# Attention scores with positive sign, high parts as plain copies, eight heads' query copies on GpSimd, loads of values and weights spaced

## The chip, the cores and the metric

The kernel runs on one core of a Trainium2 chip. The metric is device time in microseconds (us) of one execution, as the median of several runs. The core has TensorE (PE in the profile, with its weight loads as PEld), VectorE (DVE), ScalarE (ACT), GpSimd (POOL) and SyncE (SP, which here issues nearly all DMAs).

## The reference

Attention with a cumulative gate, then a dense mixture of eight experts whose gate is balanced by eight Sinkhorn steps:

```python
scores = scale * np.matmul(q, k.transpose(0, 1, 3, 2))        # 4 batches, 8 heads, 576 rows, 64 wide
cum = np.cumsum(np.maximum(s, 0.0), axis=-1)
bias = -(cum[:, :, :, None] - cum[:, :, None, :])
scores = np.where(causal, -1000000000.0, scores + np.minimum(bias, 0.0))
attn = np.exp(scores - np.max(scores, axis=-1, keepdims=True))
attn = attn / (np.sum(attn, axis=-1, keepdims=True) + 1e-09)
x = attn @ v                                                  # to 2304 rows of 512
P = np.exp(x @ w_gate - max)                                  # 8 rounds: rows, then columns to sum 1
for e in range(8):
    out += P[:, e:e + 1] * (np.maximum(x @ w1[e], 0.0) @ w2[e])   # 512 -> 1024 -> 512
```

## The kernel before

All products run in a rounded fp32 form (fp32r); a number is kept as a high part and a low part (its rest), and a product is built from high times high, high times low and low times high.

**Attention** takes the first 350 us. There are 32 heads in 16 groups of two (group g holds heads 2g and 2g+1), and a group has five slots of 128 query rows (the last has 64 of both heads). The loop over `ti` starts slot `ti` (`st0`: scores on TensorE, row minimum on VectorE in `row_min`, exponential on ScalarE), and in the same pass does later steps of earlier slots: `st1` scales by the reciprocal row sum, `st2` transposes on TensorE and copies to SBUF on VectorE, `st3` multiplies with the values `vt` into `pv`. Scores are held with a minus sign, so that the maximum is a minimum; the mask adds 8e9.

**A head is prepared** in `prep_head(h)`, called in slots 1 and 3 of the group before its own. Its raw queries and keys (`rawq`, `rawk`, each 64 rows loaded twice, into partitions 0 to 63 and 64 to 127) become: `qa` (line 418, VectorE: minus the queries, rounded, on 128 partitions; for odd heads as two instructions of 512 and 64 columns), `ka` (line 423, VectorE: the keys times a column `sgn` of +1 and -1), then the low parts on GpSimd (line 428 into `kb`, line 432 into the upper half of `qa`), and a DMA `qb<-qa` (line 426) that copies the high part of the queries. Four rows of the gates reach `qb` and `kb` by small DMAs (lines 413, 416). The buffers `qa0` to `qa3` serve head h as number h mod 4. `load_head(h + 2)` (lines 334, 335) follows.

**Values** are loaded by `load_v(g + 1)` (lines 446, 449) into one of two buffers `vt`, in slot 3 of group g; the buffer must be free of the `pv` products of group g - 1.

**Weights of the early experts' pieces** are loaded as `wraw` (line 616, two loads of 512 KB for a piece u) and split into high parts on ScalarE (line 110) and low parts on GpSimd (line 111). For the first two pieces this is done in slots 4 to 17 of the loop: both loads in the first of seven slots, the four splits in the last four.

**The rest** (350 us to the end) is the experts' work in a scheme of products of sums of blocks (lines 962, 1083, 1138 for the matmuls).

A scheduler orders the instructions of each engine when the program is built, by its own estimate of durations, so an edit in one place can move instructions of all engines near it. Each engine and the SP queue then run their instructions strictly in that order; one that waits holds up all behind it.

Of the kernel before, what the change touches and what calls it, by code (L numbers as in the profile page):

```python
# [8 lines left out]
F32 = mybir.dt.float32  # L9
F32R = mybir.dt.float32r  # L10
AF = mybir.ActivationFunctionType
ALU = mybir.AluOpType
AX = mybir.AxisListType

P = 128
B, H, S, D = 4, 8, 576, 64
# [8 lines left out]
MASKED = 8e9  # L25
# [20 lines left out]
def fused_kernel(ctx: ExitStack, tc: tile.TileContext, qT, kT, v, s, w_gate, wu, out):  # L46
    nc = tc.nc

    const = ctx.enter_context(tc.tile_pool(name="const", bufs=1))
# [57 lines left out]

    def split(dst, lo, src, eng=None):

        nc.scalar.copy(dst, src)  # L110
        (eng or nc.gpsimd).tensor_tensor(
            out=lo, in0=src, in1=dst.bitcast(F32), op=ALU.subtract
        )

    def split_piece(u, pc, raw):
        if pc % 2 == 0:
            t = "w1" if pc < 2 else "w2"
            wts[u, t] = wpool.tile([P, 2, 1024], F32R, name=t, tag=t)
        w = wts[u, "w1" if pc < 2 else "w2"]
        sl = slice(pc % 2 * 512, (pc % 2 + 1) * 512)  # L120
        split(w[:, 0, sl], w[:, 1, sl], raw)

# [206 lines left out]
    def load_head(h):  # L329
# [12 lines left out]

    sgn = const.tile([P, 1], F32, name="sgn")
    nc.gpsimd.memset(sgn[:D], 1.0)
    nc.gpsimd.memset(sgn[D:], -1.0)

    crow_d = dram.tile([B * H, 6, S], F32, name="crow_d")
    cum = apool.tile([B * H, S], F32, name="cum", tag="T", bufs=7)
    cr = stage.tile([B * H, 6, S], F32R, name="cr", tag="w7")
    nc.gpsimd.memset(cr[:, 0:2, :].bitcast(F32), 1.0)  # L350
    nc.gpsimd.memset(cr[:, 4:6, :].bitcast(F32), -1.0)
    nc.vector.tensor_scalar(
# [13 lines left out]
        out=mask,  # L366
        in_=mask,
        compare_op=ALU.is_ge,
        fill=MASKED,
        base=384,  # L370
# [31 lines left out]
    def prep_head(h):  # L402
# [9 lines left out]
        for i, o, n in at:  # L412
            nc.sync.dma_start(
                out=qb[D : D + 4, o : o + n].bitcast(F32), in_=rows[:, 2:6, i : i + n]
            )
        nc.sync.dma_start(out=kb[D : D + 4, :].bitcast(F32), in_=rows[:, 0:4, :])
        for i, o, n in at:
            nc.vector.tensor_scalar(
                out=qa[:, o : o + n], in0=rq[:, i : i + n], scalar1=-1.0, scalar2=None,
                op0=ALU.mult,  # L420
            )
        with tc.issue_after(gates_done.ins) if h < 2 else ExitStack():
            nc.vector.tensor_scalar(
                out=ka, in0=rk, scalar1=sgn[:, 0:1], scalar2=None, op0=ALU.mult
            )
            nc.sync.dma_start(out=qb[:D].bitcast(F32), in_=qa[:D].bitcast(F32))
            lo = nc.vector if h < 2 else nc.gpsimd
            lo.tensor_tensor(
                out=kb[:D], in0=rk[:D], in1=ka[:D].bitcast(F32), op=ALU.subtract
            )  # L430
            for i, o, n in at:
                lo.tensor_tensor(
                    out=qa[D:, o : o + n], in0=rq[D:, i : i + n],
                    in1=qa[D:, o : o + n].bitcast(F32), op=ALU.add,
                )
# [28 lines left out]
    def row_min(T, sc, m, init, out):  # L464
        nc.vector.tensor_tensor_reduce(
            out=T, in0=sc, in1=m, scale=0.125, scalar=init,
            op0=ALU.add, op1=ALU.min, accum_out=out,
        )
# [148 lines left out]

    def w_split_early(u, pc):
        split_piece(u, pc, wraw[pc // 2][:, pc % 2 * 512 : (pc % 2 + 1) * 512])

# [45 lines left out]
    for ti in range(NS + 3):  # L666
        if ti < NS:
            g, i = slots[ti]
            if i == 3 and g + 1 < NG:
                load_v(g + 1)  # L670
            for j in heads(slots[ti]):
                st0(slots[ti], j)
# [21 lines left out]
        if 4 <= ti < 18:  # L694
            u, r = divmod(ti - 4, 7)
            if r == 0:
                w_load_early(u)
            elif r > 2:
                w_split_early(u, r - 3)
# [611 lines left out]
```

## Time and profile before

| | |
|---|---|
| median of 3 runs | 1742.1 us (1740.54 to 1746.08) |
| profiled execution, its own time | 1738.24 us |
| its span, first to last instruction | 1736.5 us |
| PE busy | 1682.0 us (97%) |
| DVE busy | 1238.2 us (71%) |
| ACT busy | 838.3 us (48%) |
| POOL busy | 855.8 us (49%) |
| mean granted TensorE clock | 0.994 of full speed |

The profiled execution's time is its span and 1.74 us around it. Busy shares are means over very different stages, so the table says which engine is the widest, not where time is lost.

### The profile page before, as it was taken

The numbers are of one execution on the slowest core, as the hardware profiler recorded it, in microseconds if no ns is written. First come the engines' busy times: TensorE is split into PE (matmuls) and PEld (weight loads), VectorE is DVE, ScalarE is ACT, GpSimd is POOL, SyncE is SP. The second block draws the span as 40 slices with busy tenths as digits, with TensorE's granted clock in tenths as the row PEclk, the third lists the DMA queues.
The fourth block names the chain that finished last, engine by engine and source line by source line (L and its number), as shares of the span: only waits on it lengthen the run. The fifth ranks groups of instructions, "written<-read, shape, count | busy, mean of one in ns | idle before, by whom it ended". The sixth has DMA issues, their size and how long they took to land.

```text
span 1736.5 us, 31221 instructions
## 1 busy us (share of the span) xinstructions
PE 1682.0 (97%) x11109; PEld 1574.6 (91%) x11109; DVE 1238.2 (71%) x2352; ACT 838.3 (48%) x1817; POOL 855.8 (49%) x761
## 2 busy tenths in 40 slices
PE   5889999999999999999999999999999999999998
PEld 4678888889889889998889999999999999999998
DVE  6867666565586766776548777877776787777775
ACT  5876666723554444444245444444445444444442
POOL 5559647612564543553314445544544454454454
PEclk9899999999999999999999999999999999999999
DMA  6667656364687767865956555565587555555552
GB/s 177 195 195 221 204 161 200 104 235 176 212 314 255 244 209 239 260 220 189 336 184 193 178 187 183 183 191 178 184 307 256 177 183 188 180 182 182 186 176 85
DMA packets 204986, 352.09 MB, mean 203 GB/s; under 512 B 21088, under 2 KB 103008, under 8 KB 204800
## 3 DMA queue, kind: packets, MB, share of 16 engines
q1 hardware_dynamic: 204512, 349.52, 62.6%
q8 instruction: 88, 1.44, 0.3%
q10 hardware_dynamic: 320, 0.59, 0.1%
q14 instruction: 66, 0.54, 0.1%
HBM read 249.94 MB, written 94.81 MB: 199 GB/s over the span
## 4 chain that ended last, share of the span: by engine, by line
PE 78%; DVE 11%; DMA 4%; issue 3%; POOL 2%; SPq 1%; ACT 1%; DVEq 0%; POOLq 0%; ACTq 0%
PE c L962 29%; PE zz L1083 13%; PE zz L1138 12%; PE y L1138 8%; PE g L148 3%; PE g L177 3%; DVE s L937 3%; PE sc L456 2%; PE pv L558 2%; DVE h L252 2%; PE tr L528 2%; PE c L148 2%; PE c L177 2%; DVE a L1066 1%; DVE z L255 1%
## 5 line engine op out<-in xcount | busy, mean ns | idle before, releaser
L252 POOL TENSOR_TENSOR w2o<-r,w2o 128x512 fp32r<-128x512 f32 x196 | 279.6, 1448 | 363.9 <-ACT w2o L1119 327.6
L962 PE MATMUL c<-xS,w1o 128*128 128x384 f32 x1344 | 278.0, 339 | 4.2 <-DVE z L255 1.7
L1138 PE MATMUL zz<-w2o,h 128*128 128x256 f32 x2016 | 280.2, 282 | 0.0
L1138 PEld LDWEIGHTS zz<-w2o,h 128*128 128x128 f32 x2016 | 269.4, 188 | 0.4 <-ACT h L925 0.2
L1083 PE MATMUL zz<-w2p,h 128*128 128x512 f32 x1008 | 256.4, 393 | 0.5 <-ACT h L925 0.4
L937 DVE SCALAR_TENSOR_TENSOR s<-z,s 128x384 f32<-128x384 f32 x224 | 207.4, 963 | 48.6 <-ACT s L1000 46.8
L925 ACT ACTIVATE h<-z 128x384 fp32r<-128x384 f32 x252 | 130.6, 525 | 223.5 <-DVE z L255 221.1
L962 PEld LDWEIGHTS c<-xS,w1o 128*128 128x128 f32 x1344 | 226.6, 188 | 8.5 <-DVE z L255 2.9
L926 DVE SCALAR_TENSOR_TENSOR h<-z,h 128x384 fp32r<-128x384 f32 x252 | 184.5, 737 | 64.1 <-ACT h L925 61.8
L1083 PEld LDWEIGHTS zz<-w2p,h 128*128 128x128 f32 x1008 | 187.1, 187 | 32.0 <-ACT h L925 0.7
L1138 PE MATMUL y<-w2o,h 128*128 128x256 f32 x1512 | 206.2, 283 | 3.7 <-DVE a L1066 3.0
L1138 PEld LDWEIGHTS y<-w2o,h 128*128 128x128 f32 x1512 | 196.5, 188 | 8.4 <-DVE a L1066 7.3
L962 PE MATMUL c<-x,w1o 128*128 128x384 f32 x1008 | 202.0, 336 | 0.0
L252 POOL TENSOR_TENSOR h<-s,h 128x384 fp32r<-128x384 f32 x112 | 137.9, 1235 | 102.6 <-ACT h L933 101.8
L255 DVE TENSOR_TENSOR z<-c,t 128x384 f32<-128x384 f32 x252 | 136.7, 549 | 55.8 <-PE c L962 48.8
L962 PEld LDWEIGHTS c<-x,w1o 128*128 128x128 f32 x1008 | 171.2, 188 | 0.1
L1066 DVE SCALAR_TENSOR_TENSOR a<-zz,prob,a 128x256 f32<-128x256 f32 (+1 forms) x210 | 110.9, 529 | 78.3 <-PE zz L1138 53.2
L933 ACT CAST h<-s 128x384 fp32r<-128x384 f32 x224 | 113.3, 514 | 96.0 <-DVE s L937 94.6
L962 PE MATMUL c<-xS,wp 128*128 128x384 f32 x672 | 134.8, 336 | 5.0 <-DVE z L255 4.4
L962 PEld LDWEIGHTS c<-xS,wp 128*128 128x128 f32 x672 | 119.5, 188 | 13.5 <-DVE z L255 4.6
L1119 ACT CAST w2o<-r 128x1024 fp32r<-128x1024 f32 x98 | 102.4, 1046 | 59.3 <-PE y L1138 49.4
L252 POOL TENSOR_TENSOR wp<-s,wp 128x512 fp32r<-128x512 f32 x56 | 80.4, 1436 | 87.1 <-ACT wp L861 81.2
(141 smaller groups left out, 2748.8 us busy)
## 6 DMA issues: line engine op xcount, KB each, us to landing
w1o<-w1d SPq DMA_DIRECT2D x392, 256.0 KB
w1d<-wp SPq DMA_DIRECT2D x84, 512.0 KB
r<-wu SPq DMA_DIRECT2D x70, 512.0 KB
r<-w2d SPq DMA_DIRECT2D x56, 512.0 KB
sa<-wu SPq DMA_DIRECT2D x28, 512.0 KB
w2d<-sb SPq DMA_DIRECT2D x56, 256.0 KB
wraw<-wu SPq DMA_DIRECT2D x22, 512.0 KB
rawq<-qT SPq DMA_DIRECT2D x64, 144.0 KB
```

Source lines behind the costliest of these rows:

```text
L148: nc.tensor.matmul(ps[:, :n], lhsT=w1[:, w, o : o + P], rhs=xcols(b, x, k, n0, n), start=(k == 0 and t == 0), stop=(k == KD - 1 and t == 2),)
L252: (eng or nc.gpsimd).tensor_tensor(out=out, in0=a, in1=b, op=ALU.subtract)
L255: (eng or nc.gpsimd).tensor_tensor(out=out, in0=a, in1=b, op=ALU.add)
L925: mark["a"] = nc.scalar.activation(t[:, 0], z, AF.Relu)
L926: mark["v"] = nc.vector.scalar_tensor_tensor(out=t[:, 1], in0=z, scalar=0.0, in1=t[:, 0].bitcast(F32), op0=ALU.max, op1=ALU.subtract,)
L933: nc.scalar.copy(t[:, 0], z)
L937: nc.vector.scalar_tensor_tensor(out=out, in0=z, scalar=0.0, in1=other, op0=ALU.max, op1=op)
L962: mm = nc.tensor.matmul(ps, lhsT=w[:, wl, k], rhs=x[:, xl, k], start=(fresh and k == 0 and t == 0), stop=(k == 1 and t == 2), skip_group_c ...
L1066: nc.vector.scalar_tensor_tensor(out=a, in0=ps, scalar=prob[:, c, e : e + 1], in1=a, op0=ALU.mult, op1=ALU.add)
L1083: mm = nc.tensor.matmul(zb[ci], lhsT=h[:, a, ci * P : (ci + 1) * P], rhs=w[:, b_], start=(ui == 0 and f == 0 and t == 0), stop=(ui == UPE ...
L1119: nc.scalar.copy(w[:, :, 0], r)
L1138: nc.tensor.matmul(ps, lhsT=h[:, a, ci * P : (ci + 1) * P], rhs=w[:, ui, b_], start=(fresh and ui == 0 and t == 0), stop=(ui == UPE - 1 an ...
```

## The change

The scores become positive: `qa` and `ka` are plain copies with rounding, `sgn` is gone, the gate rows get the other signs, the mask's fill the other sign, and the row minimum's factor becomes -0.125. The low part of the queries is a subtraction where it was an addition. For heads 2 to 9 the copy into `qa` is an instruction of GpSimd. `load_v` moves from slot 3 to slot 4. The two `wraw` loads of the first two weight pieces come in the first and the fourth of the seven slots. The parameter `hi` of the splits is new, but no call in the program sets it.

```diff
-    sgn = const.tile([P, 1], F32, name="sgn")
-    nc.gpsimd.memset(sgn[:D], 1.0)
-    nc.gpsimd.memset(sgn[D:], -1.0)
...
-    nc.gpsimd.memset(cr[:, 0:2, :].bitcast(F32), 1.0)
-    nc.gpsimd.memset(cr[:, 4:6, :].bitcast(F32), -1.0)
+    nc.gpsimd.memset(cr[:, 0:2, :].bitcast(F32), -1.0)
+    nc.gpsimd.memset(cr[:, 4:6, :].bitcast(F32), 1.0)
...
-        fill=MASKED,
+        fill=-MASKED,
...
+        hi = nc.gpsimd if 2 <= h < 10 else nc.vector
         for i, o, n in at:
-            nc.vector.tensor_scalar(
-                out=qa[:, o : o + n], in0=rq[:, i : i + n], scalar1=-1.0, scalar2=None,
-                op0=ALU.mult,
-            )
+            hi.tensor_copy(qa[:, o : o + n], rq[:, i : i + n])
         with tc.issue_after(gates_done.ins) if h < 2 else ExitStack():
-            nc.vector.tensor_scalar(
-                out=ka, in0=rk, scalar1=sgn[:, 0:1], scalar2=None, op0=ALU.mult
-            )
+            nc.vector.tensor_copy(ka, rk)
...
-                    in1=qa[D:, o : o + n].bitcast(F32), op=ALU.add,
+                    in1=qa[D:, o : o + n].bitcast(F32), op=ALU.subtract,
...
-            out=T, in0=sc, in1=m, scale=0.125, scalar=init,
+            out=T, in0=sc, in1=m, scale=-0.125, scalar=init,
...
-            if i == 3 and g + 1 < NG:
+            if i == 4 and g + 1 < NG:
                 load_v(g + 1)
...
-            if r == 0:
-                w_load_early(u)
-            elif r > 2:
+            if r in (0, 3):
+                w_load_early(u, (r // 3,))
+            if r > 2:
                 w_split_early(u, r - 3)
```

Lines after the removed ones stand up to eight higher up in the changed kernel (418 becomes 415, 423 becomes 417, 426 becomes 418, 446 becomes 438, 465 becomes 457, 616 becomes 608).

On VectorE, about 40 us into the program, the order before is this (`qa2_214<-rawq_513` and `ka_742` belong to head 6, whose buffer `qa2` head 2 had before; `T<-sc` are row minima, `at<-tr` copies of transposed rows):

```order
L575 TENSOR_TENSOR xh_566<-pv_539,xh_566 128x64
L418 TENSOR_SCALAR qa2_214<-rawq_513 128x576
L516 RECIPROCAL rec_535<-sm_476 128x2
L423 TENSOR_SCALAR ka_742<-rawk_516,sgn_177 128x576
L533 COPY at_571<-tr_569 128x128
L465 ISA T_590,mn_591<-sc_592,mask_189 128x512
L533 COPY at_575<-tr_573 128x128
L465 ISA T_632,mn_633<-sc_635,mask_189 128x288
```

In the changed kernel the same place reads (`ka_739` belongs to head 6):

```order
L567 TENSOR_TENSOR xh_561<-pv_534,xh_561 128x64
L508 RECIPROCAL rec_530<-sm_471 128x2
L525 COPY at_566<-tr_564 128x128
L457 ISA T_585,mn_586<-sc_587,mask_186 128x512
L525 COPY at_570<-tr_568 128x128
L457 ISA T_629,mn_630<-sc_632,mask_186 128x288
L457 ISA T_629,mn_630<-sc_638,mask2_195,mn_630 128x288
L508 RECIPROCAL rec_593<-sm_516 128x2
L417 CAST ka_739<-rawk_511 128x576
```

The copy of the queries has left the engine, and that of the keys stands behind two row minima and two copies that stood behind it.

On the SP queue, 30 to 90 us into the program, three pieces before: the two weight loads ahead of head 6's raw loads (`rawq_513`), the value load in the middle of head 11's raw loads (`rawq_1105`), and the value load ahead of head 11's `qb<-qa` and of head 13's raw loads (`rawq_1357`):

```order
L616 DMA wraw_437<-wu 128x1024
L616 DMA wraw_439<-wu 128x1024
L334 DMA rawq_513<-qT 64x576
...
L334 DMA rawq_1105<-qT 64x576
L449 DMA vt0_222<-v 64x128
L335 DMA rawq_1105<-qT 64x576
...
L449 DMA vt1_224<-v 64x128
L426 DMA qb3_219<-qa3_218 64x640
L334 DMA rawq_1357<-qT 64x576
```

The same pieces in the changed kernel (`rawq_508` is head 6, `rawq_1100` head 11, `rawq_1352` head 13):

```order
L608 DMA wraw_434<-wu 128x1024
L334 DMA rawq_508<-qT 64x576
L608 DMA wraw_572<-wu 128x1024
...
L334 DMA rawq_1100<-qT 64x576
L335 DMA rawq_1100<-qT 64x576
L438 DMA vt0_219<-v 128x4x128
...
L418 DMA qb3_216<-qa3_215 64x640
L334 DMA rawq_1352<-qT 64x576
L438 DMA vt1_221<-v 128x4x128
```

One weight load now stands behind head 6's raw loads, and each value load stands behind the odd head's `qb<-qa` and the raw loads that follow it.

On GpSimd, about 45 to 65 us into the program, the order before (`rawq_624`, `rawq_751`, `rawq_865` are heads 7, 8, 9; line 111 makes low parts of weights):

```order
L428 TENSOR_TENSOR kb_743<-rawk_516,ka_742 64x576
L432 TENSOR_TENSOR qa3_218<-rawq_624,qa3_218 64x512
L432 TENSOR_TENSOR qa3_218<-rawq_624,qa3_218 64x64
L428 TENSOR_TENSOR kb_854<-rawk_627,ka_853 64x576
L111 TENSOR_TENSOR w1_913<-wraw_760,w1_913 128x512 x2
L432 TENSOR_TENSOR qa0_206<-rawq_751,qa0_206 64x576
```

And in the changed kernel (`rawq_508` is head 6, `rawq_619` head 7, `rawq_748` head 8):

```order
L420 TENSOR_TENSOR kb_740<-rawk_511,ka_739 64x576
L111 TENSOR_TENSOR w2_671<-wraw_572,w2_671 128x512
L424 TENSOR_TENSOR qa2_211<-rawq_508,qa2_211 64x576
L415 CAST qa3_215<-rawq_619 128x512
L111 TENSOR_TENSOR w2_671<-wraw_572,w2_671 128x512
L415 CAST qa3_215<-rawq_619 128x64
L420 TENSOR_TENSOR kb_847<-rawk_622,ka_846 64x576
```

The copies of the queries now stand in GpSimd's order among the low parts of keys and weights; head 7's two copies have a weight piece before and between them.

## Rows read from the trace of the kernel before

**Rows 1.** The page: busy time of TensorE, and its granted clock in 40 slices (tenths).

```profile
PE 1682.0 (97%) x11109; PEld 1574.6 (91%) x11109; DVE 1238.2 (71%) x2352; ACT 838.3 (48%) x1817; POOL 855.8 (49%) x761
PEclk9899999999999999999999999999999999999999
```

**Rows 2.** Windows by stage: start:end, length, busy us of each engine, clock, DMA.

```profile
0.00:20.00 20.00, 8.33 (x25) 6.84 (x26) 11.97 (x31) 7.59 (x22) 8.04 (x29) 1.00 0.65 164
20.00:110.00 90.00, 70.79 (x557) 56.95 (x556) 69.72 (x224) 66.97 (x197) 49.92 (x41) 0.89 0.68 190
110.00:350.00 240.00, 236.27 (x1948) 209.04 (x1948) 165.74 (x502) 157.22 (x436) 156.34 (x207) 1.00 0.61 180
```

**Rows 3.** TensorE's waits, 20 to 110 us: total, times, longest.

```profile
PE sc L456 <- DVE mn L465: 11.2, 7, 3.5
```

**Rows 4.** Timeline of TensorE: start, length, instruction, [idle before it <- releaser].

```profile
22.37 0.66 PE L528 MATMUL tr<-ident,T 128*128 128x128 f32 x2 [1.83 <-DVE at L533]
...
43.87 0.47 PE L456 MATMUL sc<-ka,qa 128*128 128x128 f32 x1 [3.19 <-DVE mn L465]
...
64.97 0.69 PE L456 MATMUL sc<-ka,qa 128*128 128x384 f32 x1 [2.93 <-DVE mn L465]
...
78.59 0.85 PE L528 MATMUL tr<-ident,T 128*128 128x128 f32 x6 [1.51 <-DVE at L533]
...
95.97 0.64 PE L456 MATMUL sc<-ka,qa 128*128 128x384 f32 x1 [3.52 <-DVE mn L465]
```

**Rows 5.** Timeline of VectorE, head preparation ahead of those waits.

```profile
20.71 1.31 DVE L418 TENSOR_SCALAR qa<-rawq 128x512 fp32r<-128x512 f32 x1 [0.45 <-DMA rawq<-qT]
...
40.70 0.46 DVE L418 TENSOR_SCALAR qa<-rawq 128x576 fp32r<-128x576 f32 x1 [2.13 <-PE tr L528]
41.61 1.40 DVE L423 TENSOR_SCALAR ka<-rawk,sgn 128x576 fp32r<-128x576 f32 x1 [0.38 <-DMA rawk<-kT]
...
62.17 2.07 DVE L418 TENSOR_SCALAR qa<-rawq 128x512 fp32r<-128x512 f32 x2 [0.48 <-DMA rawq<-qT]
...
77.55 0.56 DVE L418 TENSOR_SCALAR qa<-rawq 128x512 fp32r<-128x512 f32 x2 [1.71 <-DMA rawq<-qT]
...
92.81 2.90 DVE L418 TENSOR_SCALAR qa<-rawq 128x512 fp32r<-128x512 f32 x2 [1.67 <-DMA rawq<-qT]
```

**Rows 6.** Timeline of GpSimd at two of these places.

```profile
56.78 2.51 POOL L111 TENSOR_TENSOR w<-wraw,w 128x512 fp32r<-128x512 f32 x2 [5.94 <-ACT w L110]
...
92.98 2.66 POOL L111 TENSOR_TENSOR w<-wraw,w 128x512 fp32r<-128x512 f32 x2
```

**Rows 7.** Chain that ended last, in order of time, around 30 and 87 us.

```profile
30.40 6.25 DMA wraw<-wu
36.66 4.82 DMA rawk<-kT
...
87.62 0.51 SPq L449
```

**Rows 8.** Waits of the SP queue, 20 to 110 us.

```profile
SPq L449 <- PE pv L558: 7.1, 3, 3.2
```

**Rows 9.** Windows just behind three of TensorE's waits.

```profile
44.00:48.00 4.00, 4.00 (x22) 3.40 (x24) 2.93 (x15) 3.46 (x11) 3.14 (x4) 0.50 0.67 174
65.00:68.50 3.50, 3.50 (x14) 2.50 (x16) 2.90 (x9) 3.50 (x10) 3.35 (x4) 0.50 0.75 235
96.50:102.50 6.00, 6.00 (x25) 4.95 (x24) 3.90 (x15) 3.22 (x13) 3.59 (x4) 0.50 0.45 142
```

**Rows 10.** Groups by form, 0 to 350 us: busy us, mean ns, idle.

```profile
L428 POOL TENSOR_TENSOR kb<-rawk,ka 64x576 fp32r<-64x576 f32 x30 | 43.5, 1449 | 4.3 <-DVE ka L423 1.5 <-PE tr L528 0.9 <-PE sc L456 0.5
L279 POOL CAST sh<-sc 128x192 fp32r<-128x192 f32 x32 | 10.9, 352 | 2.4 <-DMA xd_S<-sh 2.0
L703 POOL CAST xh<-xh 128x256 fp32r<-128x256 f32 x2 | 0.7, 391 | 0.0
L428 DVE TENSOR_TENSOR kb<-rawk,ka 64x576 fp32r<-64x576 f32 x2 | 1.4, 743 | 0.0
```

More of the change, by code (lines that the diff above doesn't have):

```diff
@@ L106, in fused_kernel, with split @@
     cur = {}
-    def split(dst, lo, src, eng=None):
-        nc.scalar.copy(dst, src)
+    def split(dst, lo, src, eng=None, hi=nc.scalar.copy):
+        hi(dst, src)
         (eng or nc.gpsimd).tensor_tensor(
@@ L113, in split, with split_piece @@
         )
-    def split_piece(u, pc, raw):
+    def split_piece(u, pc, raw, hi=nc.scalar.copy):
         if pc % 2 == 0:
@@ L120, in split_piece @@
         sl = slice(pc % 2 * 512, (pc % 2 + 1) * 512)
-        split(w[:, 0, sl], w[:, 1, sl], raw)
+        split(w[:, 0, sl], w[:, 1, sl], raw, hi=hi)
     visits = []
@@ L616, in w_load_early, with w_split_early @@
             nc.sync.dma_start(out=wraw[pc], in_=wu[u, :, pc * 1024 : (pc + 1) * 1024])
-    def w_split_early(u, pc):
-        split_piece(u, pc, wraw[pc // 2][:, pc % 2 * 512 : (pc % 2 + 1) * 512])
+    def w_split_early(u, pc, hi=nc.scalar.copy):
+        split_piece(u, pc, wraw[pc // 2][:, pc % 2 * 512 : (pc % 2 + 1) * 512], hi)
     slots = [(g, i) for g in range(B * NPAIR) for i in range(5)]
```

## The prediction

> **What bounds the kernel now.** I read the page first, then stages, then TensorE's waits, then what its releasers were doing. TensorE is busy in 97% of the span and its clock is a full 9 tenths or more in all slices but one [rows 1], so nearly all of the time is TensorE's work, which this change leaves alone. Time can only be had where TensorE stands still or runs at a lower clock. The windows by stage show where [rows 2]: TensorE is idle 11.7 of the first 20 us (the first loads and the first head, whose chain keeps its steps), 90 - 70.8 = 19.2 us from 20 to 110 us at a mean granted clock of 0.89, and 3.7 us from 110 to 350 us at full clock. Behind 350 us the order of every engine is the same before and after. So the stage from 20 to 110 us decides, and 19.2 us plus what its clock costs is the most that there is.
>
> In that stage the largest wait is that of scores for the row minimum on VectorE, which frees the score banks: 11.2 us in 7 waits [rows 3]. The timeline of TensorE shows five large idle stretches, 1.83, 3.19, 2.93, 1.51 and 3.52 us, together 13.0 of the 19.2 us, all ended by VectorE [rows 4]. Just ahead of each, VectorE was not at row minima: it stood in the preparation of a head for a later group [rows 5]. For head 3 it waited 0.45 us for a DMA and then took 1.31 us for a copy of 512 columns; for head 6 it waited 2.13 us until TensorE gave back the `qa` buffer, copied, waited 0.38 us for the raw keys and took 1.40 us for them; for head 9 it waited 0.48 us and then took 2.07 us; for head 11 it waited 1.71 us; for head 13 it waited 1.67 us and took 2.90 us. The copies themselves are short: 576 columns took 0.46 us at 40.70, and the same two instructions that took 2.90 us for head 13 took 0.56 us for head 11. The long ones lie over GpSimd work: head 13's pair ended at 95.71 us, and GpSimd's pair of weight pieces, begun at 92.98, at 95.64 us [rows 5, 6]. So there are two causes: an in-order VectorE that waits for raw data or buffers, and copies that stop while GpSimd works.
>
> The raw data were late for a reason on the SP queue. The two weight loads issued from 30.40 us on landed 6.25 us later, and the raw keys of head 6 behind them took until 41.48 us [rows 7]. The value load at 87.62 us had waited for `pv` of an earlier group; such waits hold the whole queue for 7.1 us in three cases, the longest 3.2 us [rows 7, 8]. Behind them in the order stood the rest of head 11's and head 13's raw loads.
>
> **The change part by part.**
>
> *Queries' copies of heads 2 to 9 to GpSimd.* This takes 12 instructions from VectorE and gives 12 to GpSimd. What VectorE gains is its stalls. Head 3: 0.45 us of wait and 1.31 - 0.46 = 0.85 us of stopping, 1.3 us of TensorE's 1.83. Head 6: from 40.70 to the end of the keys' copy at 43.01 us VectorE does nothing for the scores; both copies leave this place (the keys' now stand behind two row minima), 2.3 less a reciprocal that stays, 2.2 of TensorE's 3.19. Head 9: 0.48 + 2.07, I take 2.5 of 2.93 [rows 4, 5].
>
> GpSimd's price for a copy of 576 columns is not in the trace. Its copies of 192 and 256 columns take 352 and 391 ns, so a further column costs 0.61 ns [rows 10]. From this I estimate 0.59 us for 576 columns, 0.55 + 0.27 = 0.82 us for 512 and 64; for four pairs of heads 5.6 us. The far bound is its two-input operation, 1.449 us for 576 columns [rows 10], or 11.6 us for the eight heads; nothing gives a lower bound than the 0.39 us of 256 columns, 3.1 us. I take 5.6, since it is the same operation as the row. GpSimd is busy 49.9 of these 90 us [rows 2]; with 5.6 more in a stage of 81 us it is busy 69%, with the far bound 76%. So as work it is hidden; as a place in a queue it may not be (below).
>
> The Trainium skill bears on this, page "SBUF — State Buffer", section "Who interferes with whom": a VectorE copy within SBUF and a GpSimd instruction share a pair of ports that one of them holds for its whole instruction while the other stands still. The trace agrees: 2.90 us against 0.56 us for the same pair, ended 0.07 us after GpSimd [rows 5, 6]. The rule speaks against this change as much as for it, since eight keys' copies stay on VectorE and meet GpSimd work that is 5.6 us longer.
>
> *Loads of values one slot later, weight loads spaced.* The SP queue then issues the odd head's `qb<-qa` and the raw loads ahead of a load that waits for `pv`, and only 512 KB ahead of head 6. Head 11's wait of 1.71 us covers TensorE's 1.51, and head 13's 1.67 us is the same kind: 1.5 + 1.7 = 3.2 us. Head 13's stopping of 2.90 - 0.56 = 2.3 us I leave in the sum, for its copies stay on VectorE and GpSimd's weight pieces stay near. The later values are wanted by `pv` five slots after their new place, so they are covered; without that cover a load's wait of up to 3.2 us [rows 8] would go to TensorE once.
>
> *Copies instead of multiplications, signs, mask, the row minimum's factor, `sgn`.* The counts of instructions are the same but for two memsets of one column, in the first 20 us where TensorE waits for data anyway. A copy on VectorE is bounded by 0.46 us, the multiplication by a constant [rows 5], and 0.743 us, an operation with two inputs [rows 10]; for the 12 keys' copies of this stage the far end is 3.4 us dearer. I take 0.46, the nearer kind, and no cost; VectorE is idle 20.3 us in the stage [rows 2].
>
> *Clock.* Behind three of the stretches the granted clock is 0.50, the lower level of 1.2 GHz, while TensorE is busy throughout: 4.0, 3.5 and 6.0 us [rows 9]. At 2.4 GHz this work would take half, so they cost 2.0, 1.75 and 3.0 us. Before each, TensorE had stood still for about 3 us; behind the stretches of 1.83 and 1.51 us no such fall shows in the windows that I read. Heads 6 and 9 would be left with 1.0 and 0.4 us of idle time, so 3.75 us more could come back; head 13's would not.
>
> *The sum.* 1.3 + 2.2 + 2.5 + 1.5 + 1.7 = 9.2 us of idle time. The clock's 3.75 us I set against waits that take the place of the removed ones: ScalarE is busy 67 of the 90 us [rows 2] and becomes the next to be late, and the scheduler has mixed the order anew. So 1738.2 us of the profiled execution becomes 1729.0. The median of the runs is 3.9 us above the profiled time, and I carry the difference over: 1742.1 - 9.2, about 1733 us.
>
> **The rivals.** *More:* all the stalls and all three clock stretches go: 9.2 + 2.3 + 2.0 + 1.75 + 3.0 = 18.3 us, or some 16 if a little returns, 1726 us. For it speaks that the stretches cause the falls of the clock; against it that head 13 still copies on VectorE.
>
> *Nothing to measure:* the stopping is only turned round. GpSimd's 5.6 us of new copies hold VectorE's copies of keys just when they are due, as GpSimd's work held the keys of head 6 for 1.40 us [rows 5]. Then 9.2 - 5.6 = 3.6 us remain, 1738 us. By the rule of that page of the Trainium skill this is what comes if every GpSimd copy meets one on VectorE. Against it: VectorE has its copies of keys later in the order, with nothing urgent right behind.
>
> *Slower:* GpSimd's queue is late. Its weight pieces wait for ScalarE, up to 5.94 us in the trace [rows 6]; before, only low parts stood behind that, now the copies of heads 7 and 9 and so their `qb<-qa` do. If both come the full 5.94 us too late for the scores, that is 11.9 us, with a lower clock behind each of some 2.0 and 1.75 us 15.6; the other heads still give 1.3 + 2.2 + 1.5 + 1.7 = 6.7, so the kernel is 8.9 us slower, 1751 us. It decides once scores wait for a query copy or its DMA by more than 9 us in all. Against it: the copies belong to the next group, two slots and more ahead.
>
> **How the numbers follow.** The forecast has a chance of 0.55, more 0.12, nothing to measure 0.21, slower 0.12. About 0.3%, 5.2 us, is what a measurement of this kernel can tell from no change. So faster 0.67, the same 0.21, slower 0.12. The predicted time is the forecast's, 1733. Its own range is 1728 (the clock's 3.75 us come back) to 1737. The range of 8 in 10 goes down to 1723, where most of the larger gain lies, and up to 1744, which takes in the third case, dearer copies on VectorE (3.4 us) and twice the idle time behind 110 us (3.7 us), and leaves most of the slower case out.
>
> **What would show it.** In the profile after, no idle stretch of TensorE of 2 us or more should lie between 30 and 90 us; VectorE should have no queries' copy from 20 to 70 us; the waits of the SP queue for `pv` should fall from 7.1 us to under 4; the mean clock from 20 us to the end of the stage should be above 0.92; GpSimd's copy of 576 columns should show about 0.6 us. I am wrong if scores wait for the queries' copies on GpSimd, if keys' copies on VectorE take 1.4 us more often than for three heads, or if the idle time moves behind 110 us.

## The result

| | before | after |
|---|---|---|
| median of the runs beside each other | 1740.7 us (6 runs, 1739.6 to 1746.1) | 1724.8 us (6 runs, 1721.0 to 1726.8) |
| profiled execution, its own time | 1738.24 us | 1726.83 us |
| ratio, 95% interval | | 0.9901 [0.9885, 0.9918] |

The kernel became 15.9 us faster by the medians, 11.4 by the two profiled executions. The measured 1724.8 us lies within the wide range of 1723 to 1744 us and under the forecast's own, 1728 to 1737; the gain is 1.7 times the 9.2 us of the sum.

The page after, its span, the busy time of TensorE and the granted clock in 40 slices, stands against [rows 1]:

```profile
span 1725.0 us, 31199 instructions
PE 1671.6 (97%) x11109; PEld 1566.0 (91%) x11109; DVE 1237.4 (72%) x2340; ACT 836.8 (49%) x1817; POOL 864.2 (50%) x771
...
PEclk9999999999999999999999999999999999999999
```

TensorE is busy 10.4 us less (1682.0 before). This was not foreseen: the change leaves TensorE's work alone. The same windows as in [rows 2], and one for all that follows:

```profile
0.00:20.00 20.00, 8.22 (x25) 6.63 (x26) 11.06 (x30) 7.39 (x21) 6.81 (x27) 1.00 0.66 162
20.00:110.00 90.00, 73.94 (x638) 61.29 (x637) 68.95 (x225) 69.88 (x206) 57.83 (x55) 0.91 0.71 192
110.00:350.00 240.00, 235.38 (x1915) 208.88 (x1915) 166.29 (x500) 155.15 (x433) 154.71 (x206) 0.99 0.60 180
350.00:1725.00 1375.00, 1354.09 (x8537) 1289.21 (x8535) 991.06 (x1588) 604.38 (x1158) 644.85 (x484) 1.00 0.65 210
```

From 20 to 110 us TensorE is now idle 90 - 73.94 = 16.1 us where it was 19.2, and the clock rose only from 0.89 to 0.91. From 110 to 350 us the idle time is 4.6 us (3.7 before). Since the kernel after is further on in its work at any of these times, windows at fixed times say what state a stretch is in, not what a stage gained (and 350 us lies ahead of attention's end). For that the same piece of work has to be found in both traces. Three such places in TensorE's timeline before (start, length, instruction): the first product of the stage behind attention, the first product of the last stage with `w1o`, and the last group of products.

```profile
375.63 2.53 PE L148 MATMUL c<-xh,w 128*128 128x256 f32 x19 [1.06 <-DVE acc L188]
...
879.33 1.21 PE L962 MATMUL c<-x,w1o 128*128 128x384 f32 x6
...
1730.68 1.96 PE L1138 MATMUL zz<-w2o,h 128*128 128x256 f32 x15
```

And after:

```profile
368.14 2.50 PE L148 MATMUL c<-xh,w 128*128 128x256 f32 x19
...
873.83 1.20 PE L954 MATMUL c<-x,w1o 128*128 128x384 f32 x6
...
1719.30 1.86 PE L1130 MATMUL zz<-w2o,h 128*128 128x256 f32 x15
```

Attention ends 375.63 - 368.14 = 7.5 us earlier. The stage between takes 503.7 us before and 505.7 after. The last stage takes 1730.68 + 1.96 - 879.33 = 853.3 us before and 847.3 after, 6.0 less, though each engine's instructions stand there in the same order in both kernels. So there are two gains of about the same size, and the prediction had only the first.

Where the last stage's 6.0 us are, the groups of TensorE by form say, taken from the first `w1o` product to the end (busy us, mean ns of one | idle before). Before:

```profile
L1138 PE MATMUL zz<-w2o,h 128*128 128x256 f32 x2016 | 280.2, 282 | 0.0
...
L1138 PE MATMUL y<-w2o,h 128*128 128x256 f32 x1512 | 206.2, 283 | 3.7 <-DVE a L1066 3.0 <-POOL w2o L252 0.6
```

After:

```profile
L1130 PE MATMUL zz<-w2o,h 128*128 128x256 f32 x2016 | 275.6, 279 | 0.9 <-ACT h L917 0.7
...
L1130 PE MATMUL y<-w2o,h 128*128 128x256 f32 x1512 | 203.2, 280 | 3.9 <-DVE a L1058 2.4 <-POOL w2o L252 0.6
```

The same 3528 products of `h` with `w2o` (columns of `w2o` move through, line 1138 before, 1130 after) take 280.2 + 206.2 = 486.4 us before and 478.8 after, 7.6 less; idle time has no part in it. What differs is where the tiles lie. `sgn`, 4 bytes per partition in a slot of 32, is gone, and every tile allocated behind it on that side of SBUF moved down 32 bytes: in the built programs `w2o` begins at byte 104512 of its partition before and at 104480 after, while `h` lies where it lay.

Back to attention. TensorE's waits from 20 to 110 us after (total, times, longest), against [rows 3]:

```profile
PE sc L448 <- DVE mn L457: 8.5, 9, 4.3
PE tr L520 <- DVE at L525: 2.7, 4, 1.4
PE sc L448 <- POOL qa L424: 1.4, 1, 1.4
PE sc L448 <- DMA qb<-qa: 1.0, 1, 1.0
```

The wait for the row minimum fell from 11.2 to 8.5 us, and half of what is left is one wait. TensorE's timeline at the idle stretches (the bracket is the idle time and its releaser), against [rows 4]:

```profile
23.22 0.47 PE L448 MATMUL sc<-ka,qa 128*128 128x128 f32 x1 [1.45 <-POOL qa L424]
...
42.07 0.38 PE L448 MATMUL sc<-ka,qa 128*128 128x256 f32 x1 [0.91 <-DVE mn L457]
...
58.12 0.30 PE L448 MATMUL sc<-kb,qb 68*128 68x128 f32 x1 [1.04 <-DMA qb<-qa]
...
69.78 0.41 PE L520 MATMUL tr<-ident,T 128*128 128x128 f32 x2 [1.40 <-DVE at L525]
...
92.56 0.69 PE L448 MATMUL sc<-ka,qa 128*128 128x384 f32 x1 [4.28 <-DVE mn L457]
```

Of the five large stretches, four are gone or under 1.5 us. The one for head 13 grew from 3.52 to 4.28 us. The queries' copies of heads 10 and 13 on VectorE, against [rows 5]:

```profile
67.85 1.09 DVE L415 CAST qa<-rawq 128x576 fp32r<-128x576 f32 x1 [2.21 <-POOL w L111]
...
86.68 5.15 DVE L415 CAST qa<-rawq 128x512 fp32r<-128x512 f32 x2
```

GpSimd at the second of them, against [rows 6]:

```profile
86.51 1.29 POOL L111 TENSOR_TENSOR w<-wraw,w 128x512 fp32r<-128x512 f32 x1
87.77 1.57 POOL L420 TENSOR_TENSOR kb<-rawk,ka 64x576 fp32r<-64x576 f32 x1
89.31 3.70 POOL L111 TENSOR_TENSOR w<-wraw,w 128x512 fp32r<-128x512 f32 x3
```

The pair of head 13's copies began at 86.68 us and ended at 91.83, while GpSimd ran its instructions one behind the other from 86.51 to 93.01 us; in [rows 5] the same pair had taken 2.90 us. The low clock moved, too. Windows behind three waits, against [rows 9]:

```profile
24.00:30.00 6.00, 5.53 (x32) 4.18 (x30) 4.70 (x14) 3.81 (x9) 3.71 (x5) 0.51 0.67 176
70.50:74.00 3.50, 3.33 (x17) 3.13 (x18) 3.50 (x18) 3.50 (x13) 1.61 (x2) 0.55 0.73 204
92.50:98.00 5.50, 5.44 (x26) 4.45 (x26) 3.46 (x15) 3.75 (x12) 3.58 (x4) 0.50 0.38 101
```

In the first two TensorE runs at about the lower level, 1.2 GHz, behind waits of only 1.45 and 1.40 us; before, no fall had shown behind 1.83 and 1.51. In the first it had been busy 1.90 of the 4 us from 20 to 24 us. The kernel before had been busy no more than that, and its clock stayed up:

```profile
20.00:24.00 4.00, 1.83 (x7) 1.03 (x6) 3.55 (x11) 1.18 (x5) 2.98 (x3) 1.00 0.64 170
```

The stretches behind heads 6 and 9 are gone, so 13.5 us at 0.50 became 15 at 0.50 to 0.55.

### The profile page after: what moved, and what is told of

It reads as the page before. It is cut to its first block, busy times and chain, and to the rows that moved or that the text cites. A ratio compares the mean times of both kernels' runs of the same rounds, so it can differ in the third digit from the quotient of the medians.

```text
span 1725.0 us, 31199 instructions
## 1 busy us (share of the span) xinstructions
PE 1671.6 (97%) x11109; PEld 1566.0 (91%) x11109; DVE 1237.4 (72%) x2340; ACT 836.8 (49%) x1817; POOL 864.2 (50%) x771
## 4 chain that ended last, share of the span: by engine, by line
PE 78%; DVE 13%; DMA 4%; issue 3%; ACT 1%; POOL 1%; SPq 0%; DVEq 0%; ACTq 0%; POOLq 0%
PE c L954 28%; PE zz L1075 13%; PE zz L1130 11%; PE y L1130 7%; PE g L177 4%; PE g L148 4%; DVE s L929 3%; PE sc L448 3%; PE pv L550 3%; DVE h L252 2%; PE tr L520 2%; PE c L177 1%; PE c L148 1%; DVE a L1058 1%; DVE h L918 1%
## 5 line engine op out<-in xcount | busy, mean ns | idle before, releaser
L1130 PE MATMUL zz<-w2o,h 128*128 128x256 f32 x2016 | 275.6, 279 | 0.9 <-ACT h L917 0.7
L1130 PEld LDWEIGHTS zz<-w2o,h 128*128 128x128 f32 x2016 | 265.3, 188 | 1.4 <-ACT h L917 1.3
```

What stands on the lines that cost most here:

```text
L1130: nc.tensor.matmul(ps, lhsT=h[:, a, ci * P : (ci + 1) * P], rhs=w[:, ui, b_], start=(fresh and ui == 0 and t == 0), stop=(ui == UPE - 1 an ...
```

## The experiments

The theories after the result: the attention stage gains because GpSimd copies the queries (the prediction, 6.0 of 9.2 us), or because the queue issues the raw loads earlier; the last stage gains because tiles lie elsewhere, against its being scatter or something that attention leaves behind. Each run is compared with the kernel before on the same chip. All of them are in the table at the end of this section; "attention" and "last stage" are read as above, and zz + y are the two groups' busy times.

**The kernel before with 32 bytes put in front.** One more tile behind the constants, so that all tiles behind it lie 32 bytes higher (`w2o` at 104544):

```diff
+    pad = const.tile([P, 1], F32, name="pad")
+    nc.gpsimd.memset(pad, 0.0)
```

> The kernel before with one more column of constants and one memset for it; the built order of every engine is otherwise unchanged, and tiles allocated after it lie 32 bytes higher, so that their addresses modulo 64 are those of the changed kernel. Theory of place: from 880 us on, where the orders of before and after are the same, the changed kernel is 5.5 us faster because sgn's 32 bytes are gone; then this kernel is 5 to 10 us faster than before (ratio 0.994 to 0.997) and its 256-column matmuls of line 1138 follow each other at 0.118 us instead of 0.1205. Theory of the attention stage alone (the prediction's): nothing changes, ratio 0.999 to 1.001.

Ratio 0.9986 [0.9974, 0.9997]. zz + y fell to 481.7 us, but the last stage took 853.1 us, as before: TensorE was busy only 2.4 us less in it (842.90 against 845.33) and idle 2.2 more. A shift by 32 bytes changes the products, and this one is worth next to nothing; the 5 to 10 us that were expected of it did not come.

**The changed kernel with the 32 bytes back.** The same two lines in the changed kernel, where they take the place of `sgn`, so that every tile has its old place (`w2o` at 104512).

> The changed kernel with one more column of constants, which puts the later tiles back at the addresses modulo 64 that they had before; the order is unchanged but for one memset. Theory of place: the gain behind 880 us is lost, ratio to before 0.993 to 0.997 instead of 0.990. Theory of the attention stage alone: ratio 0.989 to 0.991, as the changed kernel.

Ratio 0.9952 [0.9939, 0.9966], against 0.9901 [0.9885, 0.9918] without the two lines; the intervals do not overlap, and the ratios differ by 0.0051 or 8.9 us. The two groups from the first `w1o` product on:

```profile
L1133 PE MATMUL zz<-w2o,h 128*128 128x256 f32 x2016 | 280.5, 282 | 1.4 <-ACT h L920 1.4
...
L1133 PE MATMUL y<-w2o,h 128*128 128x256 f32 x1512 | 206.3, 283 | 3.7 <-DVE a L1061 3.0 <-POOL w2o L252 0.6
```

They are those of the kernel before, 486.8 us, and the last stage takes 854.1. Attention stays early (369.9 us). So about half of the change's gain is the place of the tiles, shown by putting them back without touching anything else.

**All queries' copies on VectorE.** The changed kernel without the move to GpSimd:

```diff
-        hi = nc.gpsimd if 2 <= h < 10 else nc.vector
+        hi = nc.vector
```

> The changed kernel with all copies of queries on VectorE. Prediction's theory: the stalls ahead of heads 3, 6 and 9, 6.0 us, come back; ratio to before 0.993 to 0.995. Rival, the loads' order did it all: no more than 1 us comes back, ratio 0.989 to 0.991.

Ratio 0.9916 [0.9904, 0.9928], attention ends at 368.4 us against 368.1. The part of the change to which the prediction gave 6.0 us is worth 0.3 us in the stage where it acts, and 0.0015 by ratios whose intervals overlap. The stalls for heads 3, 6 and 9 do not return. The largest stretch is again head 13's; TensorE, VectorE and GpSimd there:

```profile
92.28 1.09 PE L520 MATMUL tr<-ident,T 128*128 128x128 f32 x4 [4.13 <-DVE at L525]
```

```profile
86.46 5.21 DVE L415 CAST qa<-rawq 128x512 fp32r<-128x512 f32 x2
```

```profile
86.50 5.12 POOL L111 TENSOR_TENSOR w<-wraw,w 128x512 fp32r<-128x512 f32 x4
```

VectorE's two copies took 5.21 us and GpSimd's four weight pieces 5.12, from the same moment to the same moment.

**Loads as before.** The changed kernel with `load_v` in slot 3 and both `wraw` loads in the first slot again:

```diff
-            if i == 4 and g + 1 < NG:
+            if i == 3 and g + 1 < NG:
...
-            if r in (0, 3):
-                w_load_early(u, (r // 3,))
-            if r > 2:
+            if r == 0:
+                w_load_early(u)
+            elif r > 2:
```

> The changed kernel with the loads of values and weights where they stood before. Prediction's theory: heads 11 and 13 wait again, 3.2 us come back, ratio to before 0.991 to 0.993. Rival, the loads' order did it all: most of the attention stage's gain comes back, ratio 0.995 or more. If GpSimd's copies alone did it, ratio 0.989 to 0.991.

Ratio 0.9925 [0.9910, 0.9940]. Attention ends at 372.2 us, 4.0 later than in the changed kernel, while the last stage keeps its gain (846.7 us). The loads' order is worth more in attention than the move to GpSimd.

**The loads' order alone.** The kernel before with only the two edits just shown, the other way round.

> The loads of values and weights alone, put into the kernel before. Prediction's theory: heads 11 and 13 no longer wait for raw data, 3.2 us, and the places of tiles are as before: ratio 0.998. Rival, the loads are most of the attention stage's gain: 5 to 7 us, ratio 0.996 to 0.997.

Ratio 0.9922 [0.9899, 0.9945]. Attention ends at 368.3 us, the whole of the change's gain in this stage, with all copies on VectorE and multiplied by `sgn` as before. By the ratio this kernel gains some 13 us; its profiled execution, 1732.3 us, lies 5.9 us under the first of before and 8.5 under the mean of three (below). Part of that gap is the kernel before: its runs beside this one had a median of 1743.4 us, those beside most other kernels 1740.7 to 1741.4. The same slower runs stand behind the ratios with the signs and plain copies alone and with `w2o` moved alone by 96 bytes (before) or 32 (after), so these four are some 2 us in doubt. The window from 20 to 110 us, with a clock of 0.96, and what is left of the wait of [rows 3]:

```profile
20.00:110.00 90.00, 77.58 (x658) 64.11 (x657) 73.33 (x242) 71.06 (x208) 54.27 (x45) 0.96 0.72 199
```

```profile
PE sc L456 <- DVE mn L465: 3.0, 5, 1.6
```

VectorE's copies of the queries of heads 6, 9 and 11 in this kernel:

```profile
38.85 0.48 DVE L418 TENSOR_SCALAR qa<-rawq 128x576 fp32r<-128x576 f32 x1
...
59.98 0.61 DVE L418 TENSOR_SCALAR qa<-rawq 128x512 fp32r<-128x512 f32 x2
...
72.55 0.53 DVE L418 TENSOR_SCALAR qa<-rawq 128x512 fp32r<-128x512 f32 x2
```

None of them waits: of [rows 5], the 2.13, 0.48 and 1.71 us ahead of these copies are gone, and they take 0.48 us, and 0.61 and 0.53 for a pair, instead of 0.46, 2.07 and 0.56. Head 3's stretch of TensorE stays (1.87 us), head 13's is down to two of 1.16 and 1.56. Head 13's copy still waits for its raw queries:

```profile
87.29 1.06 DVE L418 TENSOR_SCALAR qa<-rawq 128x512 fp32r<-128x512 f32 x1 [1.56 <-DMA rawq<-qT]
```

The last stage is that of before (853.4 us, zz + y 486.6).

**Values alone, and weights alone.** The edit of `load_v` only, and then that of the `wraw` loads only, each in the kernel before.

> The kernel before with the loads of values alone in slot 4. Prediction's theory: heads 11 and 13, which stood behind a load that waits for pv, gain their 3.2 us and the others nothing; ratio 0.998. If the loads of values are the loads' whole effect: attention stage 368 us instead of 376, ratio 0.992 to 0.995.

> The kernel before with the weight loads alone spaced. Prediction's theory: head 6's raw keys come earlier, some 1 to 2 us of the wait at 43.87 us; ratio 0.999. If the weight loads are the loads' whole effect: attention stage 368 us, ratio 0.992 to 0.995.

Values: 0.9960 [0.9946, 0.9974], attention ends at 370.3 us, 5.3 earlier. Weights: 0.9980 [0.9969, 0.9992], attention 376.4 us, no earlier than before; its profiled execution, 1741.6 us, was the second slowest of twelve (median 1737.2), and shows no place for the 3.5 us of the ratio. By these profiles the values' later place is the edit that matters most in attention. With it the spaced weights add 2.0 us (368.3), less than kernels with the same order of attention differ among each other: 374.4 to 377.7 us in the kernels before with 32 to 96 bytes put in, 366.4 to 369.9 in the changed ones. So a difference of attention's end under some 3 us between two single profiles, here and above, is not told from scatter.

**Signs and plain copies alone.** The changed kernel with the last two reversions together (all copies on VectorE, loads as before).

> The signs and plain copies alone: query copies all on VectorE, loads of values and weights as before. Prediction's theory: worth nothing in the attention stage; with the last stage's 6 us by the place of tiles, ratio 0.996 to 0.997. Rival, the dropped multiplications or the new order give 2 to 4 us of the attention stage: ratio 0.993 to 0.995.

Ratio 0.9939 [0.9917, 0.9961]. Most of it is the tiles' place, which comes with `sgn`: the last stage takes 849.6 us and zz + y 478.8. Attention ends at 373.4, 2.2 us earlier than before, within that scatter. A keys' copy is a little shorter as a plain copy (mean 617 against 718 ns), which the prediction had left at nothing.

**Moving `w2o` alone.** Two kernels to see whether `w2o`'s own place decides: 96 bytes ahead of `w2o` in the kernel before, 32 bytes in the changed one (`P, 8`). No other tile of this stage moves.

```diff
+            if i == 0:
+                pad = hp[1].tile([P, 24], F32, name="pad", tag="pad", bufs=1)
+                nc.gpsimd.memset(pad, 0.0)
             w = hp[1].tile([P, UPE, 2, DH], F32R, name="w2o", tag="w2o", bufs=2)
```

> The kernel before with 96 bytes and one memset ahead of the two buffers w2o of the last stage, which nothing else moves: w2o at 104608 instead of 104512 (32 modulo 128, as in the changed kernel, instead of 64); the orders are the same. If the place of w2o itself is the cause: the pairs of w2o matmuls follow at 0.118 instead of 0.1205 us, the stage from the first w1o product to the end is 847 us instead of 853, ratio 0.996. If the place of other tiles is the cause: 853 us, ratio 0.999 to 1.001.

> The changed kernel with 32 bytes ahead of w2o alone, which puts it at 104512, as before; the orders are the same. If the place of w2o itself is the cause: the last stage is 853 us instead of 847, ratio to before 0.994. If the place of other tiles is the cause: 847 us, ratio 0.990.

Before with `w2o` at 104608: ratio 0.9947 [0.9928, 0.9966], last stage 849.5 us.

```profile
L1141 PE MATMUL zz<-w2o,h 128*128 128x256 f32 x2016 | 276.3, 281 | 0.6 <-ACT h L925 0.5
...
L1141 PE MATMUL y<-w2o,h 128*128 128x256 f32 x1512 | 203.5, 282 | 3.9 <-DVE a L1066 3.2 <-POOL w2o L252 0.6
```

After with `w2o` back at 104512: 0.9911 [0.9891, 0.9932], last stage 851.0 us.

```profile
L1133 PE MATMUL zz<-w2o,h 128*128 128x256 f32 x2016 | 278.0, 281 | 0.1
...
L1133 PE MATMUL y<-w2o,h 128*128 128x256 f32 x1512 | 205.5, 283 | 3.8 <-DVE a L1058 3.0 <-POOL w2o L252 0.6
```

Moving `w2o` and nothing else gives the kernel before 6.6 of the 7.6 us in these groups, and takes 4.7 of them from the changed kernel. `w2o`'s place carries most of the effect, but not alone: at the same 104512 the groups take 483.5 us with the other tiles 32 bytes lower and 486.4 with them where they were.

**Loads' order and `w2o`'s place together.** The kernel before with the edits of the loads and the 96 bytes, without signs and without GpSimd:

> The kernel before with the loads of values and weights moved and 96 bytes ahead of w2o, without signs, copies or GpSimd. If these two causes are the whole gain: attention stage 368 us, last stage 849 us, ratio 0.988 to 0.992, as the changed kernel. If the signs or GpSimd's copies hold a part: ratio 0.993 or more.

Ratio 0.9900 [0.9882, 0.9919], that of the change itself. Attention ends at 368.8 us, the last stage takes 848.0. The loads' order and another place of `w2o` are enough for the whole gain.

**Heads 10 to 13 to GpSimd as well.** The changed kernel with `2 <= h < 14`, aimed at head 13's stall.

> The changed kernel with GpSimd's copies for heads 2 to 13 instead of 2 to 9: takes away VectorE's long copy for head 13 ahead of TensorE's wait of 4.28 us at 92.56 us. If that copy holds TensorE: attention stage 3 to 4 us shorter and ratio 0.987 to 0.989. If another wait takes its place, as with heads 2 to 9: ratio 0.989 to 0.991.

Ratio 0.9880 [0.9862, 0.9899], the fastest of all kernels here, 1719.5 us. Attention ends at 363.6 us, 4.5 earlier than in the changed kernel. Its window from 20 to 110 us, and the wait whose longest had been 4.28 us:

```profile
20.00:110.00 90.00, 79.08 (x690) 65.30 (x690) 68.15 (x238) 74.88 (x224) 66.89 (x66) 0.94 0.76 212
```

```profile
PE sc L448 <- DVE mn L457: 4.4, 9, 0.9
```

Head 13's stall is gone, and attention's end moves by more than the scatter, while the ratio's interval overlaps that of the change. Here moving copies pays, where for heads 2 to 9 the loads had already removed most of what they waited for.

**A rule for the place?** The old byte 104512 is a multiple of 64 and the new 104480 is not. Three kernels test it: 32 and 64 bytes ahead of `w2o` in the kernel before, 64 in the changed one (`P, 8`, `P, 16`, `P, 16` in the lines above).

> The kernel before with 32 bytes put ahead of the w2o tiles alone: they begin at byte 104544 of their partition instead of 104512, so no longer at a multiple of 64. Theory A (a w2o that begins at a multiple of 64 bytes is read more slowly by TensorE, whatever the distance): the busy time of the last stage falls as with 96 bytes, zz from 280.2 to about 276.5 us and y from 206.2 to about 203.5, ratio about 0.995. Theory B (only certain places are good, no rule by 64): zz stays at 279 to 281 and the ratio at 0.998 to 1.000.

> The kernel before with 64 bytes put ahead of the w2o tiles alone: they begin at byte 104576, again a multiple of 64. Theory A (multiples of 64 are slow): no gain, zz 280.2 and y 206.2 us within 0.5, ratio 0.998 to 1.001. Theory B (any place but the old one may do): zz and y fall by 2 us or more each.

> The changed kernel with 64 bytes put ahead of the w2o tiles alone: they begin at byte 104544, not a multiple of 64, where 32 bytes (104512) had given zz 278.0 and y 205.5 us. Theory A: as in the changed kernel, zz 275.6 and y 203.2 within 0.5, ratio to the kernel before about 0.990. Theory B: zz stays near 278.

Ratios 0.9978 [0.9968, 0.9987], 0.9988 [0.9979, 0.9998] and 0.9957 [0.9942, 0.9972]. zz + y take 482.4, 482.6 and 485.1 us. A multiple of 64 (104576) does as well as its neighbour, and 104544, no multiple of 64, took 6.3 of the 7.6 us from the changed kernel, whose last stage needed 856.3 us. The rule falls. Of the places tried, the two with 480 us or less in these groups, 104480 and 104608, lie 128 bytes apart, and at the three between them it is 481.7 us or more. Whether that distance means anything was not tried; what of the place decides stays open.

**How far executions scatter.** The kernel before twice more and the changed one once, for their profiles.

> The kernel before once more, for its scatter. If the profiled execution of before was one of its faster ones (1738.2 us against a median of 1740.7 to 1743.4), the difference lies in the attention stage: its first product of the next stage starts at 377 to 380 us instead of 375.6, while the last stage (from the first w1o product on) stays at 853 us within 1 and zz at 280.2 us within 0.5. If it lies in the last stage, zz differs by more than 1 us between executions, and the place of the tiles explains less than I take it to.

> The same again: attention's end at 375 to 380 us, the last stage 853 us within 1, zz 280.2 us within 0.5.

> The changed kernel once more: attention's end at 364 to 369 us (its profiled execution was its slowest run), the last stage 847 us within 1, zz 275.6 and y 203.2 us within 0.5.

Attention is steady (376.4, 375.4 and 368.0 us), so the missing 4.5 us do not lie there. The last stage of before took 856.0 and 855.3 us against 853.3, more than the 1 us that I had allowed; zz was 280.7 and 281.2 us, and y 206.4 and 206.3. The changed kernel's stage took 847.7. So of before's three profiled executions the one first shown was the fastest; one more run of this kernel beside them took 1733.6 us, so its single runs spread from there to 1747.6. With the means of three and of two, attention gives 7.7 us, the last stage 7.3, and the stage between takes 1.3 back, for which no cause was sought: 13.7 of the 15.9 us of the medians. The rest is that both profiled executions of the changed kernel (1726.8 and 1727.5 us) lie above its median.

| kernel | ratio [95%] | attention ends | last stage | zz + y | `w2o` at |
|---|---|---|---|---|---|
| before, three executions | 1 | 375.4 to 376.4 | 853.3 to 856.0 | 486.4 to 487.5 | 104512 |
| loads' order alone | 0.9922 [0.9899, 0.9945] | 368.3 | 853.4 | 486.6 | 104512 |
| values alone | 0.9960 [0.9946, 0.9974] | 370.3 | 853.5 | 486.6 | 104512 |
| weights alone | 0.9980 [0.9969, 0.9992] | 376.4 | 854.7 | 486.6 | 104512 |
| before, all +32 bytes | 0.9986 [0.9974, 0.9997] | 375.4 | 853.1 | 481.7 | 104544 |
| before, `w2o` +32 | 0.9978 [0.9968, 0.9987] | 375.8 | 850.9 | 482.4 | 104544 |
| before, `w2o` +64 | 0.9988 [0.9979, 0.9998] | 377.7 | 852.9 | 482.6 | 104576 |
| before, `w2o` +96 | 0.9947 [0.9928, 0.9966] | 374.4 | 849.5 | 479.8 | 104608 |
| loads' order, `w2o` +96 | 0.9900 [0.9882, 0.9919] | 368.8 | 848.0 | 478.9 | 104608 |
| signs and plain copies alone | 0.9939 [0.9917, 0.9961] | 373.4 | 849.6 | 478.8 | 104480 |
| **the change**, two executions | 0.9901 [0.9885, 0.9918] | 368.0 to 368.1 | 847.3 to 847.7 | 478.8 to 479.0 | 104480 |
| without GpSimd's copies | 0.9916 [0.9904, 0.9928] | 368.4 | 847.4 | 479.0 | 104480 |
| with the loads as before | 0.9925 [0.9910, 0.9940] | 372.2 | 846.7 | 479.1 | 104480 |
| with the 32 bytes back | 0.9952 [0.9939, 0.9966] | 369.9 | 854.1 | 486.8 | 104512 |
| with `w2o` +32 | 0.9911 [0.9891, 0.9932] | 367.4 | 851.0 | 483.5 | 104512 |
| with `w2o` +64 | 0.9957 [0.9942, 0.9972] | 366.4 | 856.3 | 485.1 | 104544 |
| heads 2 to 13 on GpSimd | 0.9880 [0.9862, 0.9899] | 363.6 | 847.9 | 478.8 | 104480 |

## Why the prediction was wrong in size

**The step that failed** is "Behind 350 us the order of every engine is the same before and after. So the stage from 20 to 110 us decides". The order is the same; the time is not. The last stage's 6.0 us (7.3 by the means) were missing from the sum because the removal of `sgn` was costed as two memsets, and not as a tile whose going moves every tile behind it. This is shown: the tile's 32 bytes put back took the gain away.

**How the miss adds up.** The forecast for the profiled execution was 1729.0 us, and it took 1726.8, since the errors partly cancel: attention gained 1.7 us less than the sum, the last stage 6.0 more, and the stage between took 2.0 back. The other 6.0 of the 8.2 us between 1733 and 1724.8 come from the 3.9 us by which the median was to lie above the profiled execution: it lay 2.1 us below it. That term rested on three runs of the kernel before, and nothing said that it would carry over. The rival that named 1726 us is near by luck: it let all stalls and all low clock go, and 4.28 us of head 13's stall and 15 us of low clock stayed.

**The attention stage** gave 7.7 us against 9.2, so its total was nearly right, and its terms were not. *Queries' copies to GpSimd, 6.0 us:* mis-sized; 0.3 us with the new loads. Against the signs and plain copies alone with the old loads it is 373.4 - 372.2 = 1.2 us. Neither is clear of scatter, and both are far from 6.0. *Loads' order, 3.2 us:* mis-sized the other way; 7.3 us alone and 4.0 within the change. The two terms were added as if heads 3, 6 and 9 stalled for where their copies stood, and heads 11 and 13 for the queue. The trace had said more: in [rows 5] heads 6 and 9, too, began with a wait, and with the loads alone these waits are gone, and head 9's long copy with them; only head 3's stall stays for GpSimd to take. The edits remove the same stalls twice, and a stall can be counted once. Head 6's wait was read wrongly, as one for a buffer that TensorE gives back. [rows 5] put its end down to a transposition, which reads no `qa`; the last scores ahead of it began at 39.02 us, the copy at 40.70, and by the trace's semaphore records the raw queries had landed at 40.49. In four of six other executions with the same order the wait ends with their load, as in the second one of the kernel before:

```profile
39.69 0.68 DVE L418 TENSOR_SCALAR qa<-rawq 128x576 fp32r<-128x576 f32 x1 [1.42 <-DMA rawq<-qT]
```

With the weights alone, where one 512 KB load less stands ahead of these queries, there is no wait:

```profile
39.03 0.72 DVE L418 TENSOR_SCALAR qa<-rawq 128x576 fp32r<-128x576 f32 x1
```

So it, too, was a wait for a load, which the loads' order removes. TensorE's stretch behind it, 3.19 us in [rows 4], was 1.09 and 2.70 us in the other two executions, so one profile was a thin ground for its 2.2 us.

**Head 13.** The forecast let its wait for raw data go (1.7 us) and its stopping stay (2.3 us). In the changed kernel the wait is gone and the stopping is 4.6 us (5.15 against 0.56), so the stretch grew; with the loads' order alone the wait stays (1.56 us). The Trainium skill, page "SBUF — State Buffer", section "Who interferes with whom", has a copy on VectorE and a GpSimd instruction exclude each other for whole instructions. The trace agrees, and shows it over several instructions in a row: a pair of copies lasted as long as four weight pieces (5.21 and 5.12 us without GpSimd's copies).

**Clock.** The 3.75 us set against new waits were not seen as a gain from 20 to 110 us: the mean is 0.91 (0.89 in the second profiled execution), under the 0.92 named. The falls behind heads 6 and 9 are gone and two others came, behind waits under 1.5 us. With the loads alone it is 0.96. The term was rightly left out of the sum.

**GpSimd's price.** 721, 695 and 236 ns for 576, 512 and 64 columns, and the keys' copies on VectorE:

```profile
L417 DVE CAST ka<-rawk 128x576 fp32r<-128x576 f32 x32 | 19.7, 617 | 1.7 <-DMA rawk<-kT 1.7
...
L415 POOL CAST qa<-rawq 128x576 fp32r<-128x576 f32 x4 | 2.9, 721 | 13.6 <-DMA rawq<-qT 11.6 <-issue 1.9
...
L415 POOL CAST qa<-rawq 128x512 fp32r<-128x512 f32 x4 | 2.8, 695 | 0.3
...
L415 POOL CAST qa<-rawq 128x64 fp32r<-128x64 f32 x4 | 0.9, 236 | 0.0
```

Four of each make 6.6 us against 5.6. The estimate from 192 and 256 columns was 15% low; nothing hung on it. Scores waited 1.0 us for a query's DMA and 1.4 us for a low part in the same queue, far from the 9 us from which the slower rival would decide.

**The signs it named.** No idle stretch of 2 us from 30 to 90 us: right. No queries' copy on VectorE from 20 to 70 us: right for heads 2 to 9, head 10's came at 67.85. The queue's waits for `pv` under 4 us: wrong, by one wait of 6.0:

```profile
SPq L438 <- PE pv L550: 6.4, 2, 6.0
```

It ended with the value load issued at 105.44 us, and TensorE's waits for a DMA sum to 1.0 us from 20 to 110 us. Keys' copies of 1.4 us for more than three heads: one of 1.42 us and three of 1.17 to 1.33 from 20 to 72 us.

## What to carry to other kernels

When an edit removes or adds a tile, however small, compare the addresses of all tiles before and after, and count the products that read them as touched, even where the order of every instruction is the same; to measure an edit, put a tile of the same size in its place. Count a stall once: follow it to what was late first, and where two edits would both remove it, give the time to one of them. Cut by pieces of work that both traces share, not by windows at fixed times, before saying which stage gained.

## What was not expected of the hardware

The same products in the same order took 478.8 to 487.5 us by the place of tiles in SBUF alone, and within 1.1 us the same in every kernel with the same places (seven executions with the old ones, six with the new). Both `w2o` and some other tile of the stage have a part in it. The Trainium skill, page "SBUF — State Buffer", section "Who interferes with whom", says that TensorE never waits for another engine; by that no other engine's accesses to SBUF would be behind it. Whether that holds here, and whether TensorE's own reads are the cause, no run here shows.

The clock fell to its lower level behind waits of 1.45 and 1.40 us that ended at 23.22 and 69.78 us, where behind 1.83 and 1.51 us before it did not; the last wait alone does not tell whether it falls.
